# Transposing a part of the probability blocks by crossbar DMAs instead of on TensorE, in a fused attention and expert kernel

## Chip, cores and metric

One core of one Trainium2 chip. The metric is device microseconds of that core for one launch, the median of the runs. The profile is one execution more, recorded with the hardware profiler.

## What is computed

Three layers in a row, all in float32 to the caller: a banded attention with sinks, a mixture of four attention experts, and a mixture of eight feed-forward experts, of which each token uses one.

```python
scores = scale * np.matmul(q, k.transpose(0, 1, 3, 2))
keep = is_sink | in_window          # 4 sinks, window of 128
a = np.exp(np.where(keep, scores, -1e9) - max); a = a / (a.sum + 1e-09)
x = np.matmul(a, v)                 # 2 batches, 8 heads, 768 tokens, 64 wide
for e in range(4):                  # second attention, causal
    a = softmax(scale * (x @ wq[e]) @ (x @ wk[e]).T + causal)
    out += gate[e] * (a @ (x @ wv[e]) @ wo[e])
h = np.maximum(out @ w1[e_tok], 0)  # expert stage, one expert a token
result = p[e_tok] * (h @ w2[e_tok])
```

## The kernel before

The 2 x 768 tokens are cut into twelve tiles (b, i) of 128. For each tile the first attention (`p1_unit`, four units of two heads) computes scores on TensorE, adds the mask and takes the row maximum on VectorE (L687), makes exponentials on ScalarE into a float32 tile P in SBUF (L697), and then has to bring each 128x128 block of P into transposed form, since a matmul contracts over partitions. The second attention (`p2_unit`, two units of two experts a tile, about four tiles behind) does the same with i + 1 blocks an expert.

The code for that is in `unit`. Up to four blocks go together: TensorE transposes them against an identity into one PSUM bank (L721), ScalarE copies the bank to float16 (hi, L724), VectorE subtracts hi from the bank and writes the rest as float16 (lo, L728), and TensorE multiplies both halves with v in three matmuls a block (L736 to L738, "PV" below). Two banks' worth of hi and lo are a slot of the ring "pT", which has four. In a tile with sinks VectorE also copies eight sink columns of P (L706) for a common small matmul (L838).

GpSimd splits v into two halves (L636, L639, L645), splits weights, and copies sink columns of k (L573). SP issues the loads of q, k, v and weights (L422 and others) and the stores of the second attention's result (x2d, L1036). After the last tile, near 262 us, the expert stage runs to the end.

The order of the work isn't written by hand. Each step is a `Task` with an engine, an estimated duration, its dependencies, the ring slots it takes and gives back, and a priority. `Order.run` picks, step by step, the task that can start first by its own account: `LAT` holds the time from an engine's end to the next engine's start (0.14 to 0.2 us between engines, 2.0 us after a DMA). What it picks is written out, so every engine's queue is fixed at build time, and on the chip semaphores alone decide when a step starts. `add("DMA", ...)` puts work on SP's queue.

## Time and profile before

| | us |
|---|---|
| median of 3 runs | 440.16 (440.1 to 441.19) |
| profiled execution, its own time | 440.41 |
| its span, first to last instruction | 438.6 |
| TensorE busy | 420.7 |
| VectorE busy | 352.2 |
| ScalarE busy | 323.1 |
| GpSimd busy | 129.9 |

The granted TensorE clock is 0.995 on average. The execution's time holds 1.8 us around the span. Busy times of TensorE are modelled and overlap from matmul to matmul, so its share says little; starts are better. The chain of waits is followed back from the last instruction, and its shares say where a shorter step could shorten the whole.

### The profile page before, as it was taken

Reading aid. Unit: us, or ns where it says so; the run is one execution under the profiler, and the core shown is the slowest. Engines: PE = TensorE matmul, PEld = TensorE weight load, DVE = VectorE, ACT = ScalarE, POOL = GpSimd, SP = SyncE. Lnnn points to the kernel's source line nnn. Section 1 sums busy time; section 2 is a strip of 40 time slices with the busy share of each in tenths; the row PEclk is TensorE's granted clock in tenths of the full one; section 3 lists DMA queues with packets and bytes.
Section 4 is the critical chain, followed back from the end, with each engine's and each line's share of the span. In section 5 each row is a group of like instructions: output and inputs, shape, how many; then the busy total and the mean of one; then the engine's idle time right before and its main releaser. Section 6 shows DMA issues by size and latency. Waiting matters only on the chain.

```text
span 438.6 us, 10515 instructions
## 1 busy us (share of the span) xinstructions
PE 420.7 (96%) x3486; PEld 329.7 (75%) x3486; DVE 352.2 (80%) x1019; ACT 323.1 (74%) x759; POOL 129.9 (30%) x214
## 2 busy tenths in 40 slices
PE   8899999999999999999989999999999989999994
PEld 4679988769889779977966767655666767888883
DVE  3999696987889599868879887946779789998690
ACT  5799695975887598768556743936969789899780
POOL 8199921446002024110295104401102033100101
PEclk9999999999999999999999999999999999999999
DMA  8987251210210000100181025778565994100011
GB/s 173 174 189 195 53 118 49 49 50 1 75 50 1 25 2 2 49 1 27 55 315 41 26 73 172 259 240 266 193 212 188 340 390 143 49 26 24 2 50 53
DMA packets 58590, 48.28 MB, mean 110 GB/s; under 512 B 40863, under 2 KB 42399, under 8 KB 58528
## 3 DMA queue, kind: packets, MB, share of 16 engines
q1 hardware_dynamic: 56368, 40.72, 31.7%
q0 software_dynamic: 2160, 6.82, 4.6%
q8 instruction: 29, 0.48, 0.5%
q14 instruction: 33, 0.27, 0.2%
HBM read 86.58 MB, written 6.55 MB: 212 GB/s over the span
## 4 chain that ended last, share of the span: by engine, by line
PE 56%; DVE 16%; issue 16%; ACT 6%; DMA 3%; POOL 2%; SPq 1%; POOLq 0%; another core or an unknown queue 0%; ACTq 0%; DVEq 0%
PE bank L306 9%; PE bank L308 9%; PE bank L307 8%; PE bank L721 7%; PE bank L673 6%; DVE P L687 4%; PE bank L401 3%; DVE pT L728 3%; PE bank L1640 3%; DMA xg<-x2d,gix 2%; PE bank L738 2%; PE bank L736 2%; ACT P L697 2%; PE bank L1442 2%; PE bank L737 2%
## 5 line engine op out<-in xcount | busy, mean ns | idle before, releaser
L697 ACT ACTIVATE P<-P,nm 128x260 f32<-128x260 f32 (+4 forms) x160 | 84.0, 529 | 17.7 <-DVE nm L687 16.0
L728 DVE TENSOR_TENSOR pT<-bank,pT 128x512 f16<-128x512 f32 (+1 forms) x96 | 58.0, 627 | 13.6 <-ACT pT L724 13.1
L1421 DVE TENSOR_TENSOR w<-raw,w 128x1024 fp32r<-128x1024 f32 x44 | 52.9, 1220 | 12.7 <-ACT w L1413 12.4
L724 ACT ACTIVATE pT<-bank 128x512 f16<-128x512 f32 (+1 forms) x96 | 49.1, 550 | 6.8 <-PE bank L721 5.7
L1413 ACT ACTIVATE w<-raw 128x1024 fp32r<-128x1024 f32 x44 | 45.8, 1061 | 8.0 <-DMA raw<-in_moe_w_dram 6.8
L721 PE MATMUL bank<-ident,P 128*128 128x128 f32 x344 | 50.9, 280 | 0.7 <-ACT P L697 0.3
L687 DVE CUSTOM_DVE_ANT_0 P<-bank,mask 128x260 f32<-128x260 f32 (+1 forms) x96 | 36.4, 404 | 8.1 <-PE bank L673 8.0
L721 PEld LDWEIGHTS bank<-ident,P 128*128 128x128 f32 x344 | 38.5, 142 | 4.5 <-ACT P L697 2.4
L736 PEld LDWEIGHTS <-pT 128*128 128x128 f16 x344 | 31.0, 98 | 9.0 <-ACT pT L724 2.4
L1540 POOL DMA_INDIRECT out_dram<-yof,six x12 | 13.8, 1150 | 67.5 <-ACT yof L1537 66.3
L738 PEld LDWEIGHTS <-pT 128*128 128x128 f16 x344 | 30.7, 98 | 4.0 <-DVE pT L728 3.8
L673 PE MATMUL bank<-kT,qT 64*128 64x260 f32 (+1 forms) x192 | 31.2, 408 | 1.9 <-POOL kT L573 1.1
L737 PEld LDWEIGHTS <-pT 128*128 128x128 f16 x344 | 31.2, 99 | 1.1 <-issue 0.3
L697 ACT ACTIVATION_READ_ACCUMULATOR P<-P,nm 128x1 f32 x160 | 31.2, 195 | 0.0
L1462 POOL DMA_INDIRECT xgf<-x2d,gix x9 | 11.2, 1246 | 62.1 <-PE bank L1442 56.6
L306 PE MATMUL bank<-xT,wqk_h 128*128 128x256 f32 x96 | 28.8, 300 | 0.0
L401 PE MATMUL bank<-ident,raw 128*128 128x128 f32 x168 | 28.3, 289 | 0.2
L308 PE MATMUL bank<-xT,wqk_l 128*128 128x256 f32 x96 | 27.1, 282 | 0.0
L307 PE MATMUL bank<-xT,wqk_h 128*128 128x256 f32 x96 | 27.0, 281 | 0.0
L636 POOL TENSOR_SCALAR raw<-raw,s_sv 128x256 f32<-128x256 f32 x20 | 18.7, 946 | 27.1 <-DVE si_sv L532 17.7
L1421 DVE TENSOR_TENSOR xT<-raw,xT 128x1024 fp32r<-128x1024 f32 x17 | 20.6, 1216 | 6.9 <-ACT xT L1413 6.8
L401 PEld LDWEIGHTS bank<-ident,raw 128*128 128x128 f32 x168 | 20.4, 162 | 7.1 <-DVE nm L687 1.7
(444 smaller groups left out, 1319.9 us busy)
## 6 DMA issues: line engine op xcount, KB each, us to landing
raw<-in_moe_w_dram SPq DMA_DIRECT2D x104, 512.0 KB
qw<-in_moe_w_dram SPq DMA_DIRECT2D x64, 256.0 KB
raw<-in_v_dram SPq DMA_DIRECT2D x12, 256.0 KB
x2d<-x SPq DMA_DIRECT2D x12, 256.0 KB
raw<-in_q_dram SPq DMA_DIRECT2D x11, 256.0 KB
raw<-in_k_dram SPq DMA_DIRECT2D x11, 256.0 KB
raw<-in_moe_wv_dram SPq DMA_DIRECT2D x1, 512.0 KB
raw<-in_moe_wq_dram SPq DMA_DIRECT2D x1, 512.0 KB
```

What stands on the lines that cost most here:

```text
L306: nc.tensor.matmul(o, l[0], r[0], start=start, stop=False)
L307: nc.tensor.matmul(o, l[0], r[1], start=False, stop=False)
L308: nc.tensor.matmul(o, l[1], r[0], start=False, stop=stop)
L401: nc.tensor.transpose(p[:, j * 128:(j + 1) * 128], src(j), ident)
L673: nc.tensor.matmul(o, l, r, start=True, stop=True)
L687: nc.vector.tensor_tensor_reduce(p, s, sg["mask"], 0.0 if dead and st == 1 else -scale, gr["nm"] if si else 3.0e38, op0=OP.add, op1=OP.min ...
L697: nc.scalar.activation(p, p, AF.Exp, bias=gr["nm"], scale=-1.0, accum_out=sg["sum"]())
L721: nc.tensor.transpose(R[tk][:, j * 128:(j + 1) * 128], R[gr["P"]][:, c:c + 128], ident)
L724: nc.scalar.activation(R[sk_][0][:, :n * 128], R[tk][:, :n * 128], AF.Copy)
L728: nc.vector.tensor_sub(pl[:, :n * 128], R[tk][:, :n * 128], ph[:, :n * 128])
L1413: nc.scalar.activation(R["w", u, c, hf][0], R["raw", u, c, hf], AF.Copy)
L1421: eng.tensor_sub(wl[:, :, s_], R["raw", u, c, hf][:, :, s_], f32(wh)[:, :, s_])
```

## The change

Some units get the mark `xbar`: in the first attention units 0 and 2 of every tile from (0,3) on, in the second all units up to tile (1,1). In those, the order of splitting and transposing is turned round. ScalarE makes hi out of P itself, in SBUF (L764 of the changed kernel); GpSimd subtracts and writes lo beside it (L769); one DMA on SP's queue transposes hi and lo together through the crossbar into a slot of "pT" (L772), in lots of up to four blocks; and PV reads that (L780 to L782). GpSimd also copies the sink columns of these units (L718). The P of such units lies in a ring of its own with eight places, "PX", or, where it is wide, in "P" as before; hi and lo before the DMA lie in "PH", the four halves in which weights were staged. The DMA gets an estimated duration of 1.35 us and a latency of 2.7. The memory of "PX" is given back before the expert stage and used for its first tiles (`turnover`), whose first gather now waits for the last lo. The other units go as before (L809, L812, L816).

```diff
@@ -47,6 +47,9 @@
 FIT = 0.05
 NP = 5
 NPT = 4
+XB = ((0, 3), (1, 1))
+XLAT = 2.7
+NPX = 8
 NW = 5
 RPO = 30
 FILL = 0.5
@@ -101,7 +105,7 @@
                 return None
-            e = max(e, d.end + (self.SAME.get(t.eng, 0.0) if d.eng == t.eng else self.LAT[d.eng]))
+            e = max(e, d.end + (self.SAME.get(t.eng, 0.0) if d.eng == t.eng else d.lat or self.LAT[d.eng]))
         kinds = [a[0] for a in t.acq]
@@ -151,7 +155,7 @@
                 tag, k = self.held.pop(name)
-                self.slots[tag][k] = t.end + self.LAT[t.eng]
+                self.slots[tag][k] = t.end + (t.lat or self.LAT[t.eng])
             todo.remove(t)
@@ -262,7 +266,10 @@
     flat = ([128, XC], F32)
-    PW = max(S, 2 * SW) if banded else S
+    GW = 2 * BS
+    blocks_ = ExitStack()
+    px = blocks_.enter_context(tc.tile_pool(name="px", bufs=1, side="right"))
+    PW = max(S, 2 * GW) if banded else S
     bufs = {
@@ -270,7 +277,9 @@
         "P": ring(work, NP if banded else 4, "P", ([128, PW], F32)),
-        "pT": ring(work, NPT if banded else 3, "pT", ([128, 512], F16), ([128, 512], F16)),
+        "pT": ring(work, NPT if banded else 3, "pT", ([128, 1024], F16)),
+        "PH": [t.bitcast(F16) for t in half[:4]],
+        "PX": ring(px, NPX, "PX", ([128, 2 * GW], F32)),
         "x": [half[13].rearrange("p (h d) -> p h d", h=H)], "y": [raw[7][:, 6 * C:6 * C + E1 * D].rearrange("p (e d) -> p e d", e=E1)],
@@ -499,6 +508,7 @@
         join([K["wos", t] for t in range(2)] + [a], ["wo"], prio + 2)
+        K["staged"] = [K["wos", t] for t in range(2)] + [x for n in ("wv", "wq", "wk") for x in K[n, "s"]]
 
@@ -656,6 +666,8 @@
                 off = 0
+            elif st == 1 and banded:
+                off = gi * GW
             gr["P"] = ("P", *uk, gi if un.get("apart") else 0)
@@ -671,7 +683,7 @@
                     nc.tensor.matmul(o, l, r, start=True, stop=True)
-            ps = dict.fromkeys(("P", gr["P"]) for gr in groups) if si == 0 else {}
+            ps = dict.fromkeys((un.get("ring", "P"), gr["P"]) for gr in groups) if si == 0 else {}
             ts.append(add("PE", (d_m4(max(sg["w"] for sg in sgs)) + 0.004) * (1 if len(sgs) < 3 else len(sgs) / 2), sc,
@@ -702,14 +714,90 @@
         p_users = []
         if un.get("sinks"):
             def sk():
-                P2 = R[groups[0]["P"]][:, :2 * SW].rearrange("p (g w) -> p g w", g=2)
-                nc.vector.tensor_copy(un["sinks"](), P2[:, None, :, C:C + ns].to_broadcast([128, 3, 2, ns]))
-            K["sk", *key] = add("DVE", 0.08, sk, deps=exps, prio=prio)
+                P2 = R[groups[0]["P"]][:, :2 * GW].rearrange("p (g w) -> p g w", g=2)
+                (nc.gpsimd if un.get("xbar") else nc.vector).tensor_copy(un["sinks"](), P2[:, None, :, C:C + ns].to_broadcast([128, 3, 2, ns]))
+            K["sk", *key] = add("POOL" if un.get("xbar") else "DVE", 0.2, sk, deps=exps, prio=prio)
             p_users.append(K["sk", *key])
         blocks = [(gr["off"] + c, vt, gr["o"], vk, gr) for gr in groups for (c, vt, vk) in gr["blocks"]]
         ends = {gr["P"]: n for n, (_, _, _, _, gr) in enumerate(blocks)}
         pvs = []
         ok = ("O", st, key[0], key[1])
+        if un.get("xbar"):
+            n_ = len(blocks) // 2
+            if st == 1 or n_ <= 2:
+                lots = [[(0, 2 * n_)]]
+            elif n_ <= 4:
+                lots = [[(0, n_)], [(n_, n_)]]
+            else:
+                lots = [[(0, 4)], [(n_, 4)], [(4, n_ - 4), (n_ + 4, n_ - 4)]]
+            last_ = {}
+            for n, lot in enumerate(lots):
+                for a, m in lot:
+                    for x in blocks[a:a + m]:
+                        last_[x[4]["P"]] = n
+            for n, lot in enumerate(lots):
+                bl = [x for a, m in lot for x in blocks[a:a + m]]
+                w = 128 * len(bl)
+                tk, sk_ = ("PH", *uk, n), ("pT", *uk, n)
+                first = un.get("opens") and n == 0
+
+                def parts(lot=lot):
+                    at = 0
+                    for a, m in lot:
+                        c, gr = blocks[a][0], blocks[a][4]
+                        P_ = R[gr["P"]]
+                        if st == 1:
+                            m2 = m // 2
+                            v_ = P_[:, :2 * GW].rearrange("p (g k c) -> p g k c", g=2, k=2)[:, :, :m2, :128]
+                            yield v_, slice(at, at + m * 128), dict(g=2, k=m2)
+                        else:
+                            yield P_[:, c:c + m * 128], slice(at, at + m * 128), None
+                        at += m * 128
+
+                def shaped(t, dims):
+                    return t if dims is None else t.rearrange("p (g k c) -> p g k c", **dims)
+
+
+                def hi(tk=tk, parts=parts):
+                    for p_, s_, dims in parts():
+                        o_ = shaped(R[tk][:, s_], dims)
+                        nc.scalar.activation(o_, p_, AF.Copy)
+
+                def lo(tk=tk, w=w, parts=parts):
+                    ph, pl = R[tk][:, :w], R[tk][:, w:2 * w]
+                    for p_, s_, dims in parts():
+                        nc.gpsimd.tensor_sub(shaped(pl[:, s_], dims), p_, shaped(ph[:, s_], dims))
+
+                def tr(tk=tk, sk_=sk_, w=w):
+                    nc.sync.dma_start_transpose(R[sk_][:, :2 * w].rearrange("p (a c) -> p a c", c=128), R[tk][:, :2 * w])
+
+                def pv(bl=bl, sk_=sk_, w=w):
+                    ph, pl = R[sk_][:, :w], R[sk_][:, w:2 * w]
+                    for j, (_, vt, o, _, _) in enumerate(bl):
+                        oa, start = o()
+                        vh, vl = vt()
+                        s_ = slice(j * 128, (j + 1) * 128)
+                        nc.tensor.matmul(oa, ph[:, s_], vh, start=start, stop=False, skip_group_check=True)
+                        nc.tensor.matmul(oa, ph[:, s_], vl, start=False, stop=False, skip_group_check=True)
+                        nc.tensor.matmul(oa, pl[:, s_], vh, start=False, stop=True, skip_group_check=True)
+                done = list(dict.fromkeys(x[4]["P"] for x in bl if last_[x[4]["P"]] == n))
+                more = 0.07 * (len(lot) - 1)
+                h = add("ACT", d_a(w) + 0.1 + more, hi,
+                        deps=list(dict.fromkeys(x[4]["ex"] for x in bl)) + K["staged"], acq=[("PH", tk)], prio=prio)
+                l = add("POOL", 0.05 + w * 2.2 / 1000 + more, lo, deps=[h] + (p_users if done else []), prio=prio, rel=done)
+                t = add("DMA", 1.35, tr, deps=[l], acq=[("pT", sk_)], prio=prio, rel=[tk])
+                t.lat = XLAT
+                K.setdefault("xbar", []).append(t)
+                K.setdefault("xl", []).append(l)
+                if not first:
+                    pvs = pvs + [K[ok]]
+                x = add("PE", len(bl) * 3 * 0.030, pv, deps=[t] + [K[bk[3]] for bk in bl] + pvs,
+                        acq=[("B", ok)] if first else (), prio=prio, rel=[sk_])
+                if first:
+                    K[ok] = x
+                pvs = [x]
+            K["PV" + str(st), *key] = pvs[-1]
+            return
         for j0 in range(0, len(blocks), 4):
             bl = blocks[j0:j0 + 4]
             n = len(bl)
@@ -769,6 +857,8 @@
         un = {"groups": [], "st": 1, "opens": u == 0}
+        if banded and (b, i) >= XB[0] and u % 2 == 0:
+            un["xbar"], un["ring"] = True, "PX"
         if banded:
@@ -959,7 +1049,11 @@
         v2h, v2l = v2[b]
-        un = {"groups": [], "st": 2, "opens": t == 0, "apart": True}
+        un = {"groups": [], "st": 2, "opens": t == 0, "apart": 2 * n > 2 * GW or not banded}
+        if banded and (b, i) <= XB[1]:
+            un["xbar"] = True
+            if n <= 2 * GW:
+                un["ring"] = "PX"
         for g in range(2):
@@ -1427,10 +1522,17 @@
     behind = []
-    for tag, n, shape in (("xg", 1, [128, DM]), ("hs", 2, [128, 512])):
-        bufs[tag] = ring(fw, n, tag, (shape, F32))
-    for tag, n in (("ux", 1), ("hT", 2)):
-        bufs[tag] = ring(fw, n, tag, ([128, 512], FR), ([128, 512], FR))
+    for tag in ("xg", "hs", "ux", "hT"):
+        bufs[tag] = []
+
+    def turnover():
+        blocks_.close()
+        own = ctx.enter_context(tc.tile_pool(name="own", bufs=1, side="right", reuse_waits="tile"))
+        for tag, n, tiles in (("xg", 1, [([128, DM], F32)]), ("hs", 2, [([128, 512], F32)]),
+                              ("ux", 1, [([128, 512], FR)] * 2), ("hT", 2, [([128, 512], FR)] * 2)):
+            bufs[tag] += ring(own, n, tag, *tiles)
+            order.slots[tag] = [K["turnover"].end] * n
+    K["turnover"] = add("J", 0.0, turnover, deps=K["xl"], prio=at2(B - 1, 0))
     last_sc = []
```

How this moves the queues shows in three places. The first is TensorE at the first attention's tile (0,3), just behind tile (0,2)'s sinks; of before:

```order
L838 MATMUL bank_78<-vbd_0_132,skT_0_137 128x512
L721 MATMUL bank_76<-ident,P_0_103 128x128 x4
L721 MATMUL bank_82<-ident,P_0_104 128x128 x4
L721 MATMUL bank_75<-ident,P_0_105 128x128 x4
L401 MATMUL bank_77<-ident,raw_0_89 128x128 x4
L401 MATMUL bank_81<-ident,raw_0_89 128x128 x4
L736 LDWEIGHTS pT_0_106
L736 MATMUL bank_80<-v_0_99,pT_0_106 128x64
```

And the same tile in the changed kernel, where pT_0_111 comes from a DMA:

```order
L410 MATMUL bank_75<-ident,raw_0_88 128x128 x4
L410 MATMUL bank_80<-ident,raw_0_89 128x128 x4
L685 MATMUL bank_76<-kT,qT_0_95 128x260
L685 MATMUL bank_77<-kT,qT_0_95 128x260
L685 MATMUL bank_78<-k_0_213,q_0_125 128x256
L685 MATMUL bank_79<-k_0_213,q_0_125 128x256
L685 MATMUL bank_82<-kT,qT_0_95 128x260
L685 MATMUL bank_81<-kT,qT_0_95 128x260
L780 LDWEIGHTS pT_0_111
L780 MATMUL bank_76<-v_0_102,pT_0_111 128x64
```

The transposes of this unit are gone, and scores of the next tile (L685 with qT) and of the second attention (L685 with q) stand ahead of its PV. In all TensorE's queue holds 180 transposes of P instead of 344, and is otherwise the same in number.

The second place is SP's queue at the same time, in the changed kernel; raw_0_87 to raw_0_89 are the tiles of v, q and k:

```order
L431 DMA raw_0_87<-in_v_dram 128x8x64
L772 DMA_TRANSPOSE pT_0_111<-raw_0_83 128x8x128
L772 DMA_TRANSPOSE pT_0_112<-raw_0_83 128x8x128
L431 DMA raw_0_88<-in_q_dram 128x8x64
L431 DMA raw_0_89<-in_k_dram 128x8x64
L772 DMA_TRANSPOSE pT_0_109<-raw_0_84 128x4x128
L772 DMA_TRANSPOSE pT_0_112<-raw_0_84 128x8x128
L431 DMA raw_0_87<-in_v_dram 128x8x64
```

46 transposing DMAs now stand between the loads and stores: 34 of 8 blocks (hi and lo of four), 4 of 6 and 8 of 4.

The third is GpSimd's queue in the changed kernel, in the second batch, where it splits v (v_0 and v_1 are its halves) and makes lo (raw_0_83 and raw_0_84 are "PH"):

```order
L769 TENSOR_TENSOR raw_0_84<-P_0_106,raw_0_84 128x512
L718 COPY skp_0_140<-PX_0_119 128x3x8
L769 TENSOR_TENSOR raw_0_83<-P_0_105,raw_0_83 128x128
L769 TENSOR_TENSOR raw_0_83<-P_0_106,raw_0_83 128x128
L649 CAST v_0_102<-raw_0_86 128x512
L655 TENSOR_TENSOR v_1_103<-raw_0_86,v_0_102 128x256 x2
L769 TENSOR_TENSOR raw_0_83<-PX_0_119,raw_0_83 128x512
L646 TENSOR_SCALAR raw_0_87<-raw_0_87,s_sv_1624 128x256 x2
L769 TENSOR_TENSOR raw_0_84<-P_0_108,raw_0_84 128x512
```

Subtractions (L769) stand both ahead of and behind the steps that split v (L646, L649, L655), of which the cast waits for a buffer of the ring of v. ScalarE's queue has 50 copies to hi (L764) in place of 46 out of PSUM; VectorE's has 46 subtractions and 14 copies fewer.

## Rows read from the trace of the kernel before

**Rows 1.** The page, part 1: busy us, share of the span, instructions.
```profile
PE 420.7 (96%) x3486; PEld 329.7 (75%) x3486; DVE 352.2 (80%) x1019; ACT 323.1 (74%) x759; POOL 129.9 (30%) x214
```

**Rows 2.** Four stretches (us), the first three: busy (x), PEclk, DMA share, GB/s.
```profile
core 0: us, PE busy (x) PEld busy (x) DVE busy (x) ACT busy (x) POOL busy (x), PEclk, DMA share, GB/s
0.00:60.00 60.00, 56.04 (x530) 44.13 (x531) 47.25 (x185) 47.56 (x152) 44.85 (x110) 1.00 0.73 153
60.00:215.00 155.00, 152.68 (x1666) 129.68 (x1665) 129.72 (x528) 117.75 (x371) 32.36 (x46) 1.00 0.12 32
215.00:262.00 47.00, 44.09 (x417) 33.11 (x416) 39.10 (x147) 28.36 (x70) 20.66 (x31) 0.96 0.33 119
```

**Rows 3.** The chain of waits inside 60 to 215 us, shares by line.
```profile
by line: PE bank L673 14.1%; PE bank L721 12.2%; PE bank L306 10.9%; PE bank L308 9.7%; PE bank L307 9.5%; PE bank L401 6.3%; DVE P L687 5.7%; DVE pT L728 4.6%; PE bank L738 3.9%; PE bank L736 3.6%; ACT P L697 3.3%; PE bank L737 3.1%; ACT p
```

**Rows 4.** TensorE: start, us, count; L721 by form (busy, mean ns); L721 by stretch.
```profile
110.14 1.04 PE L721 MATMUL bank<-ident,P 128*128 128x128 f32 x8
111.02 0.60 PE L401 MATMUL bank<-ident,raw 128*128 128x128 f32 x4
...
L721 PE MATMUL bank<-ident,P 128*128 128x128 f32 x344 | 50.9, 280 | 0.7 <-ACT P L697 0.3 <-DVE nm L687 0.2
...
60.00:215.00 155.00, 31.95 (x218) 23.85 (x216) 1.00 0.12 32
```

**Rows 5.** VectorE by form: count, busy us, mean ns; the copy within 60 to 215.
```profile
L728 DVE TENSOR_TENSOR pT<-bank,pT 128x512 f16<-128x512 f32 x76 | 50.4, 684 | 12.1 <-ACT pT L724 11.6
L728 DVE TENSOR_TENSOR pT<-bank,pT 128x256 f16<-128x256 f32 x20 | 8.2, 414 | 1.6 <-ACT pT L724 1.6
...
L706 DVE COPY skp<-P 128x24 f32<-128x24 f32 x22 | 3.8, 178 | 0.0
```

**Rows 6.** ScalarE by form: hi out of PSUM, and a copy out of SBUF.
```profile
L724 ACT ACTIVATE pT<-bank 128x512 f16<-128x512 f32 x76 | 42.6, 594 | 4.9 <-PE bank L721 3.8 <-DVE xT L311 0.7
L724 ACT ACTIVATE pT<-bank 128x256 f16<-128x256 f32 x20 | 7.5, 383 | 1.9 <-PE bank L721 1.9
...
L493 ACT ACTIVATE wo_h<-raw 128x512 fp32r<-128x512 f32 x2 | 1.2, 619 | 0.0
```

**Rows 7.** GpSimd by form: subtractions of two widths, and a small copy.
```profile
L645 POOL TENSOR_TENSOR v<-raw,v 128x256 f16<-128x256 f32 x20 | 13.1, 674 | 0.8
...
L497 POOL TENSOR_TENSOR wo_l<-raw,wo_h 128x512 fp32r<-128x512 f32 x2 | 2.4, 1178 | 0.0
...
L573 POOL COPY kT<-kT 128x16 f32<-128x16 f32 x10 | 1.6, 196 | 2.5 <-PE bank L673 2.5
```

**Rows 8.** Waits of GpSimd, 60 to 215 us: total, times, longest.
```profile
POOL v L639 <- PE bank L738: 34.6, 2, 25.2
POOL v L639 <- issue: 24.4, 1, 24.4
```

**Rows 9.** SP from 74 us, and three windows of 1 us (columns as in rows 2).
```profile
74.05 0.37 SPq L422 DMA_DIRECT2D raw<-in_k_dram  x1
...
75.00:76.00 1.00, 1.00 (x19) 0.61 (x15) 1.00 (x4) 0.77 (x2) 1.00 (x2) 1.00 0.84 193
76.00:77.00 1.00, 0.70 (x5) 0.20 (x2) 1.00 (x5) 1.00 (x5) 0.93 (x2) 1.00 0.31 69
77.00:78.00 1.00, 0.96 (x8) 0.93 (x9) 1.00 (x6) 0.89 (x3) 0.91 (x2) 1.00 0.00 0
```

**Rows 10.** VectorE by form, 30 to 57 us, then 105 to 158 us.
```profile
L728 DVE TENSOR_TENSOR pT<-bank,pT 128x512 f16<-128x512 f32 x8 | 5.2, 683 | 0.5 <-ACT pT L724 0.4
L706 DVE COPY skp<-P 128x24 f32<-128x24 f32 x8 | 3.1, 392 | 0.3 <-ACT P L697 0.2
L852 DVE SCALAR_TENSOR_TENSOR r<-sums 128x8 f32<-128x8 f32 x2 | 0.9, 466 | 0.0
...
L728 DVE TENSOR_TENSOR pT<-bank,pT 128x512 f16<-128x512 f32 x18 | 12.1, 685 | 4.5 <-ACT pT L724 4.4
L706 DVE COPY skp<-P 128x24 f32<-128x24 f32 x5 | 0.9, 178 | 0.0
L852 DVE SCALAR_TENSOR_TENSOR r<-sums 128x8 f32<-128x8 f32 x3 | 0.5, 161 | 0.3 <-ACT P L697 0.3
```

**Rows 11.** TensorE's weight loads of PV that wait for lo: total, times, longest.
```profile
PEld L738 <- DVE pT L728: 3.8, 10, 0.8
```

More of the change, by code (lines that the diff above doesn't have):

```diff
@@ L63 @@
 class Task:
-    __slots__ = ("eng", "dur", "fn", "deps", "acq", "rel", "prio", "end", "name", "rows", "fills")
+    __slots__ = ("eng", "dur", "fn", "deps", "acq", "rel", "prio", "end", "name", "rows", "fills", "lat")
     def __init__(self, eng, dur, fn, deps, acq, rel, prio, rows=False):
@@ L71, in __init__ @@
         self.fills = False
+        self.lat = None
 class Order:
@@ L723, in hi @@
             def hi(tk=tk, sk_=sk_, n=n):
-                nc.scalar.activation(R[sk_][0][:, :n * 128], R[tk][:, :n * 128], AF.Copy)
+                nc.scalar.activation(R[sk_][:, :n * 128], R[tk][:, :n * 128], AF.Copy)
             def lo(tk=tk, sk_=sk_, n=n):
-                ph, pl = R[sk_]
+                ph, pl = R[sk_][:, :512], R[sk_][:, 512:]
                 nc.vector.tensor_sub(pl[:, :n * 128], R[tk][:, :n * 128], ph[:, :n * 128])
             def pv(bl=bl, sk_=sk_):
-                ph, pl = R[sk_]
+                ph, pl = R[sk_][:, :512], R[sk_][:, 512:]
                 for j, (_, vt, o, _, _) in enumerate(bl):
@@ L1380, in fused_kernel @@
     last += [K["xT", B - 1, i] for i in range(NT)] + [K["wos", t] for t in range(2)]
+    last += K["xbar"]
     spent = last + [K["v2p", B - 1, i] for i in range(NT)] + [K["qkp", B - 1, m, c] for m in range(4) for c in range(NT // 2)]
@@ L1463, in ga @@
                                          in_offset=bass.IndirectOffsetOnAxis(ap=gix[:, u:u + 1] if u else gix0, axis=0))
-        g0 = K["ga", u] = fo.add("POOL", 1.4, ga, deps=[K["gix"]] + [K["out", j] for j in range(T)] + [K.get("eui")] * (u > 1) if u else [K["gix0"]] + [K["out", j] for j in range(JE)],
+        g0 = K["ga", u] = fo.add("POOL", 1.4, ga, deps=[K["gix"]] + [K["out", j] for j in range(T)] + [K.get("eui")] * (u > 1) if u else [K["gix0"]] + [K["out", j] for j in range(JE)] + [K["turnover"]],
                     acq=[("xg", ("xg", u))], prio=bp - 50 if u else at2((JE - 1) // NT, (JE - 1) % NT, E1) + RPO + 6)
```

## Prediction, made before the result was known

> **What bounds the kernel now.** I read the page's busy shares first, then a table of four stretches, then the chain of waits inside the second stretch, and last the single operations that the change touches. The page shows TensorE busy 96% of the span, VectorE 80%, ScalarE 74% and GpSimd 30% [rows 1]. The first number deceives: the records of matmuls overlap. Eight transposes that begin at 110.14 us are followed by the next matmul at 111.02 us, so one costs 0.88 / 8 = 0.110 us of the array, while a record lasts 0.280 us [rows 4].
>
> The change touches only work that lies between 60 and 215 us: the first attention from token tile (0,3) on, and the second attention up to tile (1,1). There, in 155 us, VectorE is busy 129.7 us, ScalarE 117.8 and GpSimd 32.4 [rows 2]. VectorE is thus the busiest real worker, 129.7 / 155 = 84% of the time. The chain of waits in the same stretch is split: the transposes of probability blocks (L721) hold 12.2% of it, the subtractions after them (L728) 4.6%, and the rest is projections, scores and PV matmuls [rows 3]. So no engine is the wall; TensorE sets the pace most of the time and VectorE some of it. From 262 us on the expert stage runs, which the change doesn't touch, and before 60 us no unit uses the crossbar.
>
> **What the change removes.** 164 of the 344 transposes leave TensorE: 164 x 0.110 = 18.0 us of it. All 164 belong to the 218 of the stretch [rows 4]. Of the chain, L721 has 12.2% of 155 = 18.9 us, and 164 / 218 of that is 14.2 us.
>
> VectorE loses 46 subtractions: 36 of 128x512 at 0.684 us and 10 of 128x256 at 0.414 [rows 5], or 24.6 + 4.1 = 28.7 us, and 14 of the 32 copies of the sinks' columns, 14 x 0.178 = 2.5. Together 31.2 us, so VectorE would have 129.7 - 31.2 = 98.5 us left. Of the chain, 46 / 63 of L728's 7.1 us is 5.2.
>
> **What it adds.** ScalarE makes hi in both ways. 46 copies out of PSUM leave (36 x 0.594 + 10 x 0.383 = 25.2 us); 50 copies out of SBUF come, because four lots take two instructions each. The nearest row for 128x512 out of SBUF is 0.619 us, 0.025 over the one out of PSUM [rows 6]; with that 0.025 on the slope of the PSUM rows, 32 of 512 columns, 4 of 384 (0.51), 10 of 256 (0.41) and 4 of 128 (0.30) are 19.8 + 2.0 + 4.1 + 1.2 = 27.1. ScalarE gets 1.9 us more: 119.7 us.
>
> GpSimd gets the 50 subtractions. Its rows for the same work are 0.674 us for 256 columns with a float16 result and 1.178 for 512 [rows 7]; in between and below by that slope, 0.93 for 384 and 0.42 for 128. That is 32 x 1.178 + 4 x 0.93 + 10 x 0.674 + 4 x 0.42 = 49.8 us, and 14 copies at 0.196 = 2.7. GpSimd goes from 32.4 to about 85 us. It has the room: it is busy 21% of the stretch. It works in order, though, and its casts of v already wait 25 us each for a buffer that the PV matmuls give back [rows 8]. What now stands behind such a cast waits with it; the order puts subtractions there, as the third piece of order shows, so GpSimd's room isn't all usable.
>
> SP gets 46 transposing DMAs, 34 of 256 KB, 4 of 192 and 8 of 128. They share SP with the loads of q, k and v and the stores of x2d, and a load behind a transpose waits until GpSimd has made lo. I cost that at nothing: the loads run ahead of their use now, and the DMA engines are busy 12% of the stretch [rows 2]; if that cover goes, q and k of the next tile are late. No row shows a crossbar transpose. The nearest is a load of 256 KB in 1024 pieces of 256 bytes: issued at 74.05, it keeps the engines busy 0.84 of the microsecond from 75 and 0.31 of the next, and nothing after 77 [rows 9]. So the issue-to-end time lies between 2.3 and 3 us, about 2.4. Far on the other side, were the crossbar to move 32-byte pieces at the same time per piece (1.15 x 16 / 1024 us = 18 ns), 8192 pieces on 16 engines would take 9.2 us. I take the near row, since the bytes and the engines are the same. The order allows 1.35 + 2.7 = 4.05 us for one (the constants in the diff), so at 2.4 to 4 us PV matmuls find their blocks.
>
> [...]
>
> **The sum.** Three bounds on the gain: TensorE's own 18.0 us; the chain's share, 14.2 + 5.2 = 19.4; and the busiest engine. After the change that is ScalarE with 119.7 us. If the stretch again keeps its busiest engine at work 84% of the time, as now, it lasts 119.7 / 0.837 = 143.0 us, 12.0 less than 155. I take the smallest, because with the transposes gone ScalarE, which still has to do every exponential, is what a new chain will run through. The profiled execution took 440.41 us (span 438.6); 440.4 - 12.0 = 428.4. The median of the runs shown is 440.16, 0.25 lower, so some **428 us**. Its own range: down to 418, if TensorE's 18.0 and VectorE's 5.2 of the chain both come off (440.4 - 23.2 = 417.2); up to 434, if half of 12.0 is lost.
>
> **Rivals.** [...] VectorE's small operations with all operands in SBUF take longer while GpSimd works: the copy of sinks takes 0.392 us between 30 and 57 us, where GpSimd never rests, and 0.178 between 105 and 158; the sum of L852 0.466 against 0.161. The subtraction L728, which reads PSUM, stays at 0.683 and 0.685 [rows 10]. The stretch has 528 VectorE instructions; 196 are in small groups that are mostly of this kind. If GpSimd's share rises by 52.5 / 143 = 0.37, they cost up to 196 x 0.3 x 0.37 = 22 us, and VectorE is back at 120, level with ScalarE; two such engines in one chain, and GpSimd's in-order stalls, can eat 6 to 12 us. [...] For it: the rows. Against: those operations are off the chain in most places.
>
> *The transposing DMA is late (slower than before).* The place is the first weight load of a PV group (L780): it waits for the DMA, and all of TensorE's later work stands behind it. Now such waits are short, 3.8 us in ten times [rows 11]. There are 46 such groups. If each lands 0.27 us later than the order assumes and nothing hides it, that costs 46 x 0.27 = 12.4 us: that is the point from which the change doesn't gain. At 0.5 us it is 23 us of waits, or 440.4 - 12.0 + 23 = 451; if half is hidden, 440. If SP or the crossbar needs more than 155 / 46 = 3.4 us for one, SP itself is the bound: at the far end, 9.2 us x 41 (34 + 4 x 0.75 + 8 x 0.5), the stretch alone lasts 377 us and the kernel 662. For it: no row shows the operation, and the new path has four engines in a row (ScalarE, GpSimd, SP, TensorE) where it had three. Against: 4.05 us allowed is well over the 2.4 us of the row.
>
> *More than the forecast (410 to 418 us).* With PSUM banks no longer held by transposes, scores start earlier and the other engines close up too. Nothing in the waits names a bank as the releaser, so little speaks for it.
>
> That the change doesn't do what it says is ruled out: the order of the changed kernel has 180 transposes on TensorE and 46 on SP.
>
> **Numbers.** Chances: forecast (418 to 434) 0.55; given back (434 to 441) 0.18, of which 0.07 within 0.3% of before; late DMA (over 441) 0.20, half of it under 446; more than the forecast 0.07. About 0.3%, 1.3 us, is what a measurement of this kernel can tell from no change. Faster by more: 0.55 + 0.11 + 0.07 = 0.73; within: 0.07; slower: 0.20. The range 416 to 446 leaves out some 0.05 below and 0.10 above.
>
> **What would show it.** Right: in the stretch from 60 us TensorE has 164 transposes fewer; VectorE's subtraction has 50 instructions left; GpSimd's busy time rises by about 50 us; the attentions end some 12 us earlier than 262 us; a transposing DMA ends 2 to 4 us after its issue; ScalarE is then the busiest beside TensorE. Wrong: PV weight loads that wait on a DMA for more than 10 us in total, SP busy with back-to-back transposes, VectorE's busy time that falls by less than 15 us, or an expert stage whose length changes.

## The result and the profile after

The changed kernel takes 426.92 us (median of four runs, 422.76 to 428.61) against 440.13 us before: ratio 0.968, interval 0.960 to 0.976. The prediction was 428.0 us. The profiled execution took 425.71 us, its span 424.0; the page's first part, to be read against [rows 1]:

```profile
span 424.0 us, 10371 instructions
PE 404.3 (95%) x3322; PEld 316.2 (75%) x3322; DVE 337.5 (80%) x959; ACT 322.7 (76%) x763; POOL 177.9 (42%) x278
```

TensorE has 164 instructions fewer and 16.4 us less, GpSimd 48.0 us more, ScalarE 0.4 us less. VectorE lost only 14.7 us, though 46 subtractions and 14 copies left it. The stretches of the changed kernel, against [rows 2] (the first expert gather, which fetches token rows for the expert stage, starts at 201.7 us instead of 218.1 and the second at 247.7 instead of 263.7, so the cuts move):

```profile
core 0: us, PE busy (x) PEld busy (x) DVE busy (x) ACT busy (x) POOL busy (x), PEclk, DMA share, GB/s
60.00:202.00 142.00, 138.81 (x1594) 119.38 (x1593) 117.61 (x480) 117.78 (x379) 81.33 (x109) 1.00 0.59 110
202.00:249.00 47.00, 43.74 (x404) 30.71 (x403) 40.16 (x151) 26.75 (x66) 20.33 (x31) 0.96 0.32 112
249.00:424.00 175.00, 165.70 (x851) 122.70 (x849) 134.25 (x145) 129.96 (x167) 28.77 (x25) 0.98 0.49 163
```

The starts of the gathers, before and then changed, are the first starts in these two rows:

```profile
L1462 POOL DMA_INDIRECT xg<-x2d,gix x4: 988/1255/1955, 218.1 to 416.4; - x4
L1564 POOL DMA_INDIRECT xg<-x2d,gix x4: 991/1207/1295, 201.7 to 401.8; - x4
```

TensorE's column of the stretch shows it best: it is busy 138.81 of 142 us (98%), as it was 152.68 of 155 before. The 16.4 us at the first gather (16.0 at the second) are 14.7 us at the end of the profiled execution. The expert stage, from the second gather to the end, is 1.4 us longer. A piece of 3.41 us at half of TensorE's clock (granted 0.50 instead of 1.00) lies in it, which would cost 1.7 us, half of its length, if TensorE had full work in it. That it is the cause isn't shown: in e3 below the same stage is as long (176.3 us) without such a piece. Windows around the two pieces that the changed kernel has (columns as above):

```profile
222.00:228.00 6.00, 5.49 (x37) 4.55 (x38) 5.90 (x23) 5.84 (x19) 1.22 (x2) 0.72 0.00 1
338.00:344.00 6.00, 5.33 (x16) 3.91 (x17) 5.75 (x6) 4.58 (x6) 1.50 (x1) 0.72 1.05 391
```

The kernel before has one piece too, at 229.0 us, but none that answers to the second (340.2 us, behind waits of TensorE of 1.92 and 0.67 us for ScalarE and VectorE).

The operations that moved, of the changed kernel: all forms of the subtraction that VectorE kept (L816) and those of GpSimd (L769), then hi out of SBUF on ScalarE, to be read against [rows 5 to 7]:

```profile
L816 DVE TENSOR_TENSOR pT<-bank,pT x50: 403/681/692, 9.5 to 231.8; 128x512 f16<-128x512 f32 x40, 128x256 f16<-128x256 f32 x10
L769 POOL TENSOR_TENSOR raw<-PX,raw 128x512 f16<-128x512 f32 x24 | 27.8, 1164 | 10.8 <-ACT raw L764 10.7
L769 POOL TENSOR_TENSOR raw<-P,raw 128x512 f16<-128x512 f32 x8 | 9.2, 1161 | 7.5 <-ACT raw L764 7.5
L764 ACT ACTIVATE raw<-PX 128x512 f16<-128x512 f32 x24 | 14.9, 628 | 0.0
```

The durations are near the ones that the sum used (0.684, 1.178 and 0.619 us). The durations of all forms add up to 31.5 us of subtractions left on VectorE (60.2 before), 49.4 us on GpSimd and 27.4 us of hi; the busy time is less (30.7 us for L816 by the page), since records of neighbours overlap a little.

### The profile page after: what moved, and what is told of

Same layout as the page of the kernel before. It is cut to its first block, busy times and chain, and to the rows that moved or that the text cites. A ratio compares the mean times of both kernels' runs of the same rounds, so it can differ in the third digit from the quotient of the medians.

```text
span 424.0 us, 10371 instructions
## 1 busy us (share of the span) xinstructions
PE 404.3 (95%) x3322; PEld 316.2 (75%) x3322; DVE 337.5 (80%) x959; ACT 322.7 (76%) x763; POOL 177.9 (42%) x278
## 4 chain that ended last, share of the span: by engine, by line
PE 57%; issue 19%; DVE 16%; ACT 4%; POOL 3%; POOLq 0%; another core or an unknown queue 0%; DVEq 0%; ACTq 0%
PE bank L315 10%; PE bank L317 9%; PE bank L316 9%; PE bank L685 7%; PE bank L1742 4%; PE bank L809 3%; PE bank L410 3%; DVE P L699 3%; DVE pT L816 2%; DVE PX L699 2%; PE bank L1544 2%; POOL out_dram L1642 2%; ACT P L709 1%; PE bank L1140 1%; PE bank L780 1%
## 5 line engine op out<-in xcount | busy, mean ns | idle before, releaser
L709 ACT ACTIVATE P<-P,nm 128x260 f32<-128x260 f32 (+3 forms) x100 | 53.1, 535 | 14.6 <-DVE nm L699 14.4
L769 POOL TENSOR_TENSOR raw<-PX,raw 128x512 f16<-128x512 f32 (+2 forms) x34 | 35.5, 1049 | 14.5 <-ACT raw L764 14.1
L1642 POOL DMA_INDIRECT out_dram<-yof,six x12 | 13.2, 1100 | 66.8 <-ACT yof L1639 65.9
L816 DVE TENSOR_TENSOR pT<-bank,pT 128x512 f16<-128x512 f32 (+1 forms) x50 | 30.7, 630 | 9.5 <-ACT pT L812 9.3
L685 PE MATMUL bank<-kT,qT 64*128 64x260 f32 (+1 forms) x192 | 32.0, 405 | 1.5 <-issue 1.1
L709 ACT ACTIVATE PX<-PX,nm 128x260 f32<-128x260 f32 (+4 forms) x60 | 30.5, 511 | 1.5 <-DVE nm L699 1.3
L812 ACT ACTIVATE pT<-bank 128x512 f16<-128x512 f32 (+1 forms) x50 | 26.1, 551 | 3.3 <-PE bank L809 3.0
L809 PE MATMUL bank<-ident,P 128*128 128x128 f32 x180 | 27.6, 285 | 0.6 <-ACT P L709 0.3
L699 DVE CUSTOM_DVE_ANT_0 P<-bank,mask 128x260 f32<-128x260 f32 (+1 forms) x60 | 22.3, 399 | 6.0 <-PE bank L685 5.9
L685 PEld LDWEIGHTS bank<-kT,qT 64*128 64x128 f32 x192 | 19.7, 191 | 9.1 <-issue 3.9
L646 POOL TENSOR_SCALAR raw<-raw,s_sv 128x256 f32<-128x256 f32 x20 | 18.3, 924 | 18.7 <-ACT qT L416 9.8
L410 PEld LDWEIGHTS bank<-ident,raw 128*128 128x128 f32 x168 | 20.5, 164 | 7.3 <-DVE nm L699 2.0
L1604 ACT ACTIVATE hs<-bank 128x512 f32<-128x512 f32 x24 | 14.3, 595 | 15.2 <-PE bank L317 15.2
L685 PE MATMUL bank<-k,q 64*128 64x256 f32 (+3 forms) x128 | 25.3, 468 | 0.1
```

Of the source, the lines that this page charges most:

```text
L410: nc.tensor.transpose(p[:, j * 128:(j + 1) * 128], src(j), ident)
L685: nc.tensor.matmul(o, l, r, start=True, stop=True)
L699: nc.vector.tensor_tensor_reduce(p, s, sg["mask"], 0.0 if dead and st == 1 else -scale, gr["nm"] if si else 3.0e38, op0=OP.add, op1=OP.min ...
L709: nc.scalar.activation(p, p, AF.Exp, bias=gr["nm"], scale=-1.0, accum_out=sg["sum"]())
L769: nc.gpsimd.tensor_sub(shaped(pl[:, s_], dims), p_, shaped(ph[:, s_], dims))
L809: nc.tensor.transpose(R[tk][:, j * 128:(j + 1) * 128], R[gr["P"]][:, c:c + 128], ident)
```

## The experiments

Twelve kernels were run, each with runs of the kernel before beside it. The ratios have intervals of about half a per cent each way, so many totals can't be told apart. The start of the first expert gather in the trace is a finer measure of the stretch that the change touches, but it comes from one trace each. The last column counts TensorE's pieces at half clock before the last microseconds of a run, and says on which side of that gather they lie.

| kernel | ratio to before (95%) | gather starts, us | against before | pieces of 3.41 us at half clock |
|---|---|---|---|---|
| before | 1 | 218.1 | | 1, after it |
| changed | 0.968 (0.960 to 0.976) | 201.7 | -16.4 | 2, after it |
| e1 lo on VectorE | 0.983 (0.978 to 0.987) | 208.8 | -9.3 | 2, ahead of it |
| e2 thin lo, before | 0.991 (0.987 to 0.994) | 216.4 | -1.7 | 1, after it |
| e3 first attention only | 0.983 (0.977 to 0.988) | 209.9 | -8.2 | 0 |
| e4 second only | 0.982 (0.977 to 0.986) | 210.2 | -7.9 | 0 |
| e5 no DMA | 0.969 (0.964 to 0.974) | 205.8 | -12.4 | 2, one ahead |
| e6 sinks on VectorE | 0.975 (0.971 to 0.979) | 204.9 | -13.2 | 2, one ahead |
| e7 hi on VectorE | 0.998 (0.995 to 1.002) | 218.6 | +0.4 | 3, two ahead |
| e8 three head pairs | 0.971 (0.964 to 0.979) | 205.7 | -12.4 | 4, one ahead |
| e9 thin hi | 0.968 (0.963 to 0.974) | 201.4 | -16.7 | 2, after it |
| e10 thin GpSimd lo | 0.975 (0.969 to 0.981) | 197.6 | -20.5 | 0 |
| e11 thin VectorE lo | 0.962 (0.956 to 0.968) | 200.3 | -17.8 | 0 |
| e12 lo in pieces | 0.977 (0.973 to 0.981) | 208.9 | -9.2 | 4, three ahead |

**Which relief earns the gain: e1 and e2.** The edit of e1:

```diff
-                        nc.gpsimd.tensor_sub(shaped(pl[:, s_], dims), p_, shaped(ph[:, s_], dims))
+                        nc.vector.tensor_sub(shaped(pl[:, s_], dims), p_, shaped(ph[:, s_], dims))
...
-                l = add("POOL", 0.05 + w * 2.2 / 1000 + more, lo, ...
+                l = add("DVE", d_v(w) + more, lo, ...
```

> The changed kernel with one thing undone: the 46 subtractions that make lo of the crossbar units run on VectorE again (from SBUF, instead of GpSimd); the transposes stay with the DMAs. Theory 1 (what the change bought is TensorE's 18.0 us of transposes, and VectorE's relief is worth only its 5.2 us of the chain): most of the gain stays, 427 to 433 us. Theory 2 (the gain is VectorE's relief): 437 to 441 us, as before. Theory 3 (VectorE's small operations are slowed while GpSimd works, which eats the relief): VectorE's total rises by clearly less than the 28 us that the 46 subtractions take, and the time stays within 2 us of the changed kernel's 426.9.

The edit of e2, with thin true for the units of the change:

```diff
-                nc.vector.tensor_sub(pl[:, :n * 128], R[tk][:, :n * 128], ph[:, :n * 128])
+                w = 8 if thin else n * 128
+                nc.vector.tensor_sub(pl[:, :w], R[tk][:, :w], ph[:, :w])
```

> The kernel before, with lo of the same probability blocks cut to its first 8 columns (the rest of lo is left as it was, so the products with lo are not those of the reference): VectorE loses about as much work as the change takes from it, TensorE keeps every transpose. Theory 1 (TensorE's freed time is the gain): 435 to 440 us, at most the 5.2 us that VectorE had of the chain. Theory 2 (VectorE's relief is the gain): 426 to 431 us.

e1 measured 435.16 us and e2 438.62, where before took 442.31 beside them. These are gains of 7.2 and 3.7 us. Taken off the 440.13 us that the expectations start from, they give 433.0 and 436.4 us: theory 1 holds, in e1 at the edge of its range, and theory 2 falls. VectorE's total in e1 rises from 337.5 to 349.3 us, by far less than 28, as theory 3 says, but the time doesn't stay within 2 us.

With TensorE relieved and VectorE not, the gather comes 9.3 us earlier; with VectorE relieved and TensorE not, 1.7; with both, 16.4. So TensorE's transposes are the larger part. By the gathers VectorE's relief is worth 1.7 us before they are gone and 7.1 us after. By the totals the two gains add up to 10.9 us of about 13, and the difference is less than the intervals, so that the two are worth more together isn't shown. The stretch of e2, with VectorE relieved, and then that of e1:

```profile
60.00:214.00 154.00, 152.48 (x1677) 130.02 (x1675) 115.19 (x536) 118.11 (x373) 32.55 (x47) 1.00 0.12 33
60.00:209.00 149.00, 141.59 (x1575) 119.93 (x1575) 128.82 (x530) 116.52 (x373) 37.25 (x60) 0.98 0.51 101
```

In e2 VectorE does 14.5 us less and TensorE stays at 99%. In e1 TensorE is down to 95% of the stretch, VectorE is up at 128.82 us, and the granted clock is 0.98: of the 7.1 us, two pieces at half clock (97.5 and 135.1 us, the first behind 1.3 idle microseconds of TensorE in four) can be up to 3.4.

**Which half earns it: e3 and e4.** The change's XB becomes ((0, 3), (-1, -1)) in e3 and ((9, 9), (1, 1)) in e4.

> The changed kernel with the crossbar for the first attention alone: 26 of the 46 transposing DMAs, 104 of the 164 transposes taken from TensorE, and all 14 sinks' copies on GpSimd. Theory 1 (gain in proportion to the TensorE time freed): 104/164 of 13.2 us, 8.4 us, 431 to 433 us. Rival (the loss by the third tile, some 4 us, comes with the first attention's part, and the second's part earns the gain): 435 to 440 us.

> The changed kernel with the crossbar for the second attention alone: 20 of the 46 transposing DMAs, 60 of the 164 transposes, sinks' copies on VectorE again. Theory 1 (proportion): 60/164 of 13.2 us, 4.8 us, 434 to 437 us. Rival (the first attention's part loses the 4 us seen by the third tile and the second's part earns the gain): 426 to 432 us, and the first attention's tails of the first three tiles at the times of the kernel before.

434.55 and 434.59 us: 8.2 and 7.9 us at the gather, whose sum 16.1 is near the changed kernel's 16.4. The counts in both expectations were wrong: TensorE's instructions fall from 3486 to 3418 in e3 and to 3390 in e4, so the halves have 68 and 96 transposes (18 and 28 DMAs). By these counts 6.8 and 9.6 of 16.4 us would be due; the first half gives 1.4 more and the second 1.7 less, which is no more than orders differ for other reasons (below). Both rivals fall, since each half gains about as much as the other.

**Does the DMA cost anything: e5.** The DMA's task is left out, and PV reads its tiles before the transpose.

```diff
-                def pv(bl=bl, sk_=sk_, w=w):
+                def pv(bl=bl, sk_=tk, w=w):
...
-                t = add("DMA", 1.35, tr, deps=[l], acq=[("pT", sk_)], prio=prio, rel=[tk])
+                t = l
...
```

> The changed kernel with its 46 transposing DMAs left out: the products with V read hi and lo untransposed, as soon as GpSimd has made lo (so these products are not those of the reference), and the two rings turn over at the products. Theory 1 (the transposing DMAs cost nothing: they lie beside other work): within 2 us of the changed kernel, ratio to the kernel before 0.965 to 0.973. Rival (they come late or hold SP and the DMA engines): at least 4 us faster than the changed kernel, ratio 0.960 or less, and less time in the attentions.

428.68 us, no faster than the changed kernel, as theory 1 says. (It isn't a clean comparison: its order differs, "PH" with its four places is held until the products, and it has a piece at half clock ahead of the gather, which comes 4.1 us later.) In the changed kernel itself, TensorE's weight loads waited for the transposing DMA once:

```profile
PEld L780 <- DMA pT<-raw: 0.3, 1, 0.3
L772 SPq DMA_TRANSPOSE pT<-raw x46: 1188/1236/2577, 55.0 to 179.0; - x46
```

The second row says that SP is held 1.24 us by each (46 are 57 us of its stretch). The last of them is issued alone, at 178.98 us; the windows behind it have a share of the DMA engines only from 180 us on:

```profile
179.50:180.00 0.50, 0.50 (x17) 0.50 (x14) 0.50 (x2) 0.00 (x0) 0.00 (x0) 1.00 0.00 0
180.00:180.50 0.50, 0.50 (x7) 0.50 (x6) 0.47 (x2) 0.27 (x1) 0.00 (x0) 1.00 0.65 132
180.50:181.00 0.50, 0.50 (x6) 0.43 (x5) 0.20 (x1) 0.49 (x2) 0.00 (x0) 1.00 1.12 212
181.00:181.50 0.50, 0.50 (x4) 0.30 (x4) 0.37 (x1) 0.50 (x3) 0.00 (x0) 1.00 1.17 252
181.50:182.00 0.50, 0.50 (x6) 0.35 (x4) 0.50 (x2) 0.37 (x2) 0.00 (x0) 1.00 1.03 387
```

Some 212 GB/s go on until a store of x2d joins at about 181.4 us and then goes on alone at 387. The packets of 256 bytes that are the transpose's begin 1.17 us after its issue and end at 2.58 us, and so do those of the one issued at 159.11 us, behind which SP issues nothing for 5 us. So 256 KB take about 1.4 us of transfer and 2.6 us from issue to end, near the row that the prediction took (2.4 us). The far side that it set against that row, 9.2 us with pieces of 32 bytes, shows in no run. The DMA engines' share of the stretch went from 0.12 to 0.59, and still TensorE waited for them only the 0.3 us above.

**Undoing small parts, and more of the same: e6, e7, e8.** e6 puts the 14 sinks' copies on VectorE again, e7 moves hi from ScalarE to VectorE, and e8 gives three of the four head pairs to the crossbar.

```diff
-                (nc.gpsimd if un.get("xbar") else nc.vector).tensor_copy( ...
+                nc.vector.tensor_copy( ...
...
-                        nc.scalar.activation(o_, p_, AF.Copy)
+                        nc.vector.tensor_copy(o_, p_)
...
-        if banded and (b, i) >= XB[0] and u % 2 == 0:
+        if banded and (b, i) >= XB[0] and u != 3:
```

> The changed kernel with one thing undone: the 14 sinks' copies on VectorE again, 2.5 us of its time. Theory 1 (GpSimd's queue has room, VectorE is no longer the bound): within 2 us of the changed kernel, ratio 0.966 to 0.974. Rival (GpSimd's sinks' copies, which stand behind its slow subtractions, hold up the tails of the tiles): faster by 3 us or more, ratio 0.962 or less.

> The changed kernel with hi of the crossbar units made by VectorE (a copy from SBUF to float16) in place of ScalarE, which loses some 27 us of work; VectorE gets between 10 us (its quickest copies of the trace) and 29 us (the time of its subtractions). Theory 1 as it was predicted (ScalarE sets the length of the attentions beside TensorE): 421 to 425 us, ratio 0.957 to 0.966. Rival (TensorE is the bound, and VectorE the next, as the first four runs say): no gain, ratio 0.968 to 0.985, the more the longer the copies take.

> The changed kernel with three of the four head pairs of the first attention's tiles by crossbar instead of two: 52 more transposes off TensorE (5.7 us), 13 subtractions off VectorE (8.9 us), 13 on GpSimd of 1.16 us, 13 transposing DMAs more. Theory 1 (TensorE still sets the stretch, 138.8 of 142 us busy): 4 to 5 us faster than the changed kernel, ratio 0.957 to 0.962. Rival (ScalarE, GpSimd or SP sets it by now): no faster or slower, ratio 0.968 or more.

e6: 431.07 us (ratio 0.975, just above theory 1's range); the rival falls, and the copies are no worse off on GpSimd. e7: 440.73 us, a ratio above the ranges of both theories; the whole gain is gone, though ScalarE has 101.39 us to do from 60 to 215 us where it had 117.75 before:

```profile
60.00:215.00 155.00, 146.02 (x1577) 120.72 (x1578) 137.71 (x531) 101.39 (x335) 83.85 (x109) 0.98 0.56 101
L764 DVE CAST raw<-PX 128x512 f16<-128x512 f32 x21 | 9.5, 454 | 0.1
```

VectorE is at 137.71 us, 89% of it, more than in the long stretch of any other run shown here. Since VectorE got the work that ScalarE lost, e7 can't tell whether ScalarE was the bound. e8: 430.65 us (428.57 without its slowest run, of which its trace is), no gain from the transposes taken away (34 by TensorE's count of 3288, with 9 DMAs, not the expectation's 52 and 13, so 3.7 us). All three have an order of their own, with one or two pieces at half clock ahead of the gather, so differences of 3 us between them can't be put down to the edits. The gathers of e5, e6 and e8 come 3 to 4 us later than the changed kernel's, though none of them adds work to TensorE. So some of the changed kernel's 16.4 us may be a good order and not the change; no run settles how much.

**Which engine is left as the bound: e9, e10, e11.** These keep the changed kernel's order on every engine, and thin one instruction to 8 columns (after the first full use of a buffer). e9 has hi on ScalarE, e10 lo on GpSimd, e11 the lo that stayed on VectorE (c_ and w are the 8 columns, once the buffer has been full):

```diff
-                        nc.scalar.activation(o_, p_, AF.Copy)
+                        nc.scalar.activation(o_[..., c_], p_[..., c_], AF.Copy)
...
-                        nc.gpsimd.tensor_sub(shaped(pl[:, s_], dims), p_, shaped(ph[:, s_], dims))
+                        nc.gpsimd.tensor_sub(shaped(pl[:, s_], dims)[..., c_], p_[..., c_], shaped(ph[:, s_], dims)[..., c_])
...
-                nc.vector.tensor_sub(pl[:, :n * 128], R[tk][:, :n * 128], ph[:, :n * 128])
+                nc.vector.tensor_sub(pl[:, :w], R[tk][:, :w], ph[:, :w])
```

> The changed kernel in its own order, with ScalarE's hi of the crossbar units cut to 8 columns of each block row (45 of 49 instructions; the rest of hi is left as it was, so those products are not the reference's): some 20 us of ScalarE's work gone, nothing added. Theory 1 as predicted (ScalarE is the one nearest beside TensorE): 3 us or more faster than the changed kernel, ratio 0.961 or less. Rival A (VectorE is the one nearest, as the run with hi on VectorE says): within 2 us, ratio 0.965 to 0.973.

> The changed kernel in its own order, with GpSimd's lo of the crossbar units cut to 8 columns (45 of 49 instructions; those products are not the reference's): some 40 us of GpSimd's work gone. Theory 1 (GpSimd costs nothing where it stands) and rival A: within 2 us, ratio 0.965 to 0.973. [...]

> The changed kernel in its own order, with VectorE's remaining lo subtractions cut to 8 columns (42 of 50 instructions; those products are not the reference's): some 20 us of VectorE's work gone. Rival A (VectorE is the one nearest beside TensorE): 3 to 6 us faster than the changed kernel, ratio 0.955 to 0.961. Theory 1 (ScalarE) and the reading that TensorE alone is left: within 2 us, ratio 0.965 to 0.973.

The stretch of 60 to 202 us, of e9, then e10, then e11:

```profile
60.00:202.00 142.00, 138.32 (x1599) 119.33 (x1597) 117.89 (x481) 105.21 (x380) 81.76 (x110) 1.00 0.59 111
```

```profile
60.00:202.00 142.00, 141.07 (x1652) 121.89 (x1653) 110.86 (x484) 118.66 (x381) 51.48 (x114) 1.00 0.61 119
```

```profile
60.00:202.00 142.00, 139.36 (x1609) 119.85 (x1608) 110.59 (x483) 118.92 (x379) 82.57 (x110) 1.00 0.61 113
```

e9 (426.33 us): 12.6 us less of ScalarE move the gather by 0.3 us. ScalarE doesn't set the length. e11 (423.09 us, ratio 0.962, between the two ranges expected): 7.0 us less of VectorE move it by 1.4 us, and the second gather by 3.3. Neither of the changed kernel's pieces at half clock appears in this trace, which may be a part of that. So VectorE is nearer to the bound than ScalarE, at less than half of what is taken from it. e10: the gather comes 4.1 us earlier, with 29.9 us less of GpSimd and 6.8 us less of VectorE, none of whose instructions was touched. Its total (428.38 us) can't be set beside the others: the altered values send tokens elsewhere, and its expert stage has a gather and 60 matmuls more.

So GpSimd's lo does cost something where it stands, against theory 1 and rival A: without it VectorE's operations get shorter and the stretch ends earlier. VectorE's rows for the same two operations, before, changed, e1 and e10 (count, then ns at least/median/most):

```profile
L1185 DVE TENSOR_TENSOR r_sc<-r_sc,rev x4: 164/168/174, 92.3 to 205.3; 128x16 f32<-128x16 f32 x4
L929 DVE TENSOR_SCALAR g_mx<-g_mx x5: 157/169/169, 69.3 to 213.5; 128x2 f32<-128x2 f32 x5
```

```profile
L1279 DVE TENSOR_TENSOR r_sc<-r_sc,rev x5: 164/524/2294, 87.3 to 213.0; 128x16 f32<-128x16 f32 x5
L1019 DVE TENSOR_SCALAR g_mx<-g_mx x5: 160/170/1143, 72.2 to 197.1; 128x2 f32<-128x2 f32 x5
```

```profile
L1279 DVE TENSOR_TENSOR r_sc<-r_sc,rev x4: 165/170/302, 88.7 to 195.7; 128x16 f32<-128x16 f32 x4
L1019 DVE TENSOR_SCALAR g_mx<-g_mx x5: 152/164/170, 73.7 to 206.8; 128x2 f32<-128x2 f32 x5
```

```profile
L1283 DVE TENSOR_TENSOR r_sc<-r_sc,rev x5: 167/175/525, 87.1 to 208.9; 128x16 f32<-128x16 f32 x5
L1023 DVE TENSOR_SCALAR g_mx<-g_mx x5: 160/169/169, 71.9 to 193.0; 128x2 f32<-128x2 f32 x5
```

With lo on GpSimd an instruction of 0.17 us takes up to 2.29; with lo on VectorE, or thin, at most 0.53. Added up until the second gather, the operations that both kernels have in equal number on VectorE take 8.7 us longer in the changed kernel than before, and 10.2 us less again in e10. The prediction took 31.2 us off VectorE, and 14.7 came off; 8.7 of the missing 16.5 us went here. Another part is that VectorE's records overlap (868 records of 273.2 us in all cover 217.6 us in the kernel before), so leaving one out frees less than its length.

**Shorter pieces on GpSimd: e12.** If VectorE waits only for the GpSimd instruction in progress, shorter ones should help.

```diff
+                        for c in range(0, m, 256):
+                            k_ = slice(c, min(c + 256, m))
+                            nc.gpsimd.tensor_sub(o_[:, k_], p_[:, k_], h_[:, k_])
...
```

> The changed kernel in its own order, with each of GpSimd's subtractions of 512 columns made as two of 256 (and those of 384 as 256 and 128): the same work in shorter pieces. Rival B' (VectorE's small operations between SBUF operands stand until the GpSimd instruction in progress ends): the longest of them fall from up to 2294 ns towards 700 ns, VectorE's busy time falls by 2 to 4 us, and the time by 1 to 2 us, ratio 0.963 to 0.967. Theory 1 (it costs nothing): same time, ratio 0.967 to 0.970. Against both: the pieces cost GpSimd some 5 us more in all and lo comes later, ratio 0.972 or more.

430.5 us, slower than the changed kernel (the intervals just overlap), the gather 7.2 us later. Rival B' falls: the longest operation is now 3331 ns. The ratio is that of the last case, and GpSimd's total did rise, from 177.9 to 183.3 us. The largest single loss is in the timeline of e12, VectorE and then GpSimd from 60.5 us (start, us, operation):

```profile
58.84 1.78 DVE L718 COPY skp<-P 128x24 f32<-128x24 f32 x1
60.55 3.33 DVE L1093 TENSOR_TENSOR r<-r,gate 128x4 f32<-128x4 f32 x1
63.80 0.41 DVE L699 CUSTOM_DVE_ANT_0 PX<-bank,mask 128x260 f32<-128x260 f32 x1
```

```profile
60.51 0.21 POOL L718 COPY skp<-PX 128x24 f32<-128x24 f32 x1
60.67 0.68 POOL L777 TENSOR_TENSOR raw<-PX,raw 128x256 f16<-128x256 f32 x1
61.30 1.30 POOL L655 TENSOR_TENSOR v<-raw,v 128x256 f16<-128x256 f32 x2
62.55 1.31 POOL L772 TENSOR_TENSOR raw<-PX,raw 128x256 f16<-128x256 f32 x2
```

A multiplication of 128x4 elements lasts from 60.55 to 63.88 us: through six instructions of GpSimd, until the last of them ends at 63.86, and not until the one in progress does. VectorE's next step, a row maximum of the scores (L699), is behind it, and TensorE waits 4.66 us for it, from 59.62 us. 2.1 us into that wait its granted clock falls to 0.50 (same run, columns as above):

```profile
58.00:62.00 4.00, 1.61 (x13) 1.19 (x13) 4.00 (x5) 3.43 (x14) 4.00 (x8) 0.96 1.17 164
62.00:66.00 4.00, 1.72 (x33) 1.72 (x33) 4.00 (x15) 0.39 (x1) 1.86 (x3) 0.50 0.12 20
```

In the changed kernel the same multiplication took 0.62 us, until the end of one instruction of GpSimd, though the next followed it at once:

```profile
59.71 0.62 DVE L1085 TENSOR_TENSOR r<-r,gate 128x4 f32<-128x4 f32 x1
59.71 0.60 POOL L649 CAST v<-raw 128x512 f16<-128x512 f32 x1
60.31 0.20 POOL L718 COPY skp<-PX 128x24 f32<-128x24 f32 x1
```

Most long ones of the changed kernel are of this kind. Of its eight small operations over 0.7 us in the stretch of 60 to 202 us, each ends 17 to 31 ns behind the end of an instruction of GpSimd. For seven that is the instruction in progress, and in six of these the next one was already starting. The eighth (2294 ns, at 165.3 us) went on through two more subtractions. What decides whether VectorE gets in between two instructions isn't shown.

No version beat the changed kernel with the whole computation done.

## Why the prediction was right, point by point

- **TensorE's 18.0 us, 14.2 us of them on the chain:** 164 instructions left it, its busy time fell by 16.4 us, and by 13.9 us between the two cuts of the stretch. This term carried the larger part of the gain (e1). Not all 164 lay in the stretch, as the prediction has it: the changed kernel issues its first transposing DMA at 55.0 us, and in the kernel before about 16 of the 164 ran ahead of 60 us, which makes the 14.2 about 12.8.
- **The sum by ScalarE, 119.7 / 0.837 = 143.0 us:** the step that failed. The stretch did come out near 142 us, but ScalarE doesn't set it: e9 took 12.6 us from it and won 0.3. So the 12.0 us were right by size, by luck and not by their reason. TensorE is busy 98% of the stretch before and after, and of the three bounds its own 18.0 us is the nearest to the 16.4 of the gather. That TensorE is the bound of the changed kernel is argued from this and from e9 and e11, not shown: e8, which took 34 more transposes from it, has an order of its own and won nothing.
- **VectorE's 31.2 us, 5.2 us of the chain:** the instructions went (60.2 us of subtractions became 31.5), but the busy time fell by 14.7 us, which the prediction had named as a sign against it. By the gathers the relief was worth 1.7 us alone (e2; 3.7 by the total) and 7.1 us beside the transposes' removal (e1), so 5.2 lay between.
- **GpSimd's 52.5 us, with room:** 48.0 us came. The waits of its casts of v, which the prediction feared for, fell from 59.0 us in the stretch to 0.6; it now waits for ScalarE's hi (21.7 us). No wait of TensorE in the stretch names it; what it costs goes by way of VectorE.
- **SP and the DMAs at nothing, 2.4 us each:** confirmed by 0.3 us of waits, and nothing in e5 speaks against it; one took 2.6 us. The rival of the late DMA is out.
- **Given back by VectorE's small operations (434 to 441 us):** they do take longer beside GpSimd's lo. It cost VectorE 8.7 us, not the up to 22 of the estimate, and e10 prices it, together with GpSimd's later lo, at 4.1 us of the stretch. The runs show these times and not their cause. The forecast of 434 to 441 us was too much for the whole, because it set VectorE back to 120 us and made that the bound. VectorE did come out at 117.61 us, but TensorE was busy for 138.81.
- **The expert stage, of unchanged length:** it is 1.4 us longer in the profiled execution, with one piece at half clock in it; the cause stays open. Runs of the same kernel lie between 422.76 and 428.61 us, and the one of 422.76 us has the highest mean clock of the four, 0.996 against 0.990 to 0.992.

## What to carry to other kernels

Take the sum from the engine that is busy nearly all of the stretch, even if its records overlap, and ask of every other engine what it would cost if it fell behind. Relief on two engines of one chain can be worth more together (16.4 us by the gathers) than apart (9.3 + 1.7), though the totals here don't settle it. Work that moves to GpSimd isn't free because GpSimd has room: count VectorE's small operations with all operands in SBUF that will meet it (here VectorE's took 8.7 us longer). Cutting GpSimd's instructions into shorter ones, back to back, didn't help here: one small operation stood through several of them, for 3.33 us. To find the bound of a changed kernel, thin one engine's work in the kernel's own order; kernels that a planner orders anew differ by some microseconds for other reasons.

## What the hardware showed beyond that

VectorE stood for 3.33 us in one instruction of 128x4 elements (e12), through six GpSimd instructions in a row, none of them over 0.69 us by its record. Of the eight long operations in the changed kernel's stretch, seven (0.75 to 1.14 us) ended 17 to 31 ns behind the one GpSimd instruction that was in progress; the eighth (2.29 us), and the one in e12, stood through several. VectorE's subtraction out of PSUM, beside the same GpSimd, took 692 ns at most (L816 of the changed kernel; 693 before).

TensorE's granted clock fell from 1.00 to 0.50 for pieces of 3.41 us, or twice that. Some came during or behind idle time: within a wait of 4.66 us in e12, behind waits of 1.92 and 0.67 us at 340.2 us in the changed kernel. But the piece at 224.2 us there has only waits of 0.27 us ahead of it, and behind a wait of 1.85 us at 166.2 us the clock stayed at 1.00. A piece holds back at most half of its 3.41 us, 1.7 us of TensorE's work, and the runs here have from none (e3, e4, e10, e11) to four of them.
